# Bucketed attention and a gated feed-forward: the masks of two score blocks made in one step on row quarters of TensorE, with four score slots

## The chip, the cores and the metric

The kernel runs on one core of one Trainium2 chip. The core has TensorE (PE, matrix products; PEld is its loading of weights), VectorE (DVE), ScalarE (ACT), GpSimd (POOL) and SyncE (SP); the last two mostly issue transfers here. Matrix products read SBUF and write PSUM, which has eight banks of 2 KiB per partition. The metric is the device time of one execution in microseconds, the median of several.

## The reference

Attention in which a query sees only the keys that fall into the same hash bucket, and then a feed-forward block on the result:

```python
batch, n_heads, seq, head_dim = (4, 8, 768, 64)
...
q_bits = (np.einsum('bhsd,dk->bhsk', q, proj) > 0).astype(np.int64)      # proj: 64 x 6
k_bits = (np.einsum('bhsd,dk->bhsk', k, proj) > 0).astype(np.int64)
powers = 2 ** np.arange(n_bits)
q_bucket = np.sum(q_bits * powers, axis=-1)
k_bucket = np.sum(k_bits * powers, axis=-1)
mask = q_bucket[:, :, :, None] == k_bucket[:, :, None, :]
scores = scale * np.matmul(q, k.transpose(0, 1, 3, 2))
scores = np.where(mask, scores, -1000000000.0)
scores = scores - np.max(scores, axis=-1, keepdims=True)
attn = np.exp(scores)
attn = attn / (np.sum(attn, axis=-1, keepdims=True) + 1e-09)
return np.matmul(attn, v).astype(np.float32)
...
h = x @ w_in                                       # x: 3072 x 512, w_in: 512 x 2048
sp = np.maximum(h, 0.0) + np.log1p(np.exp(-np.abs(h)))
g = h * erf(sp)
return (g @ w_out).astype(np.float32)
```

## The kernel before

The kernel has two stages, attention and feed-forward, in one program. In each, a planner (`arrange`, L120) puts the operations in order before anything is emitted: every operation has an engine, a planned cost, a rank and a list of operations it comes after, and the planner plays the engines forward and emits each operation at its planned start. Each engine then works strictly in the order of emission; what one engine must wait for on another is put in as semaphores, from the tiles that an instruction reads and writes.

**Attention** takes the 32 heads in 16 runs of two heads each (`i`, `NPAIR` = 16). The two heads `ab` = 0, 1 lie on the lower and upper 64 partitions. A run has 2 halves of the queries (`HS` = 384 columns) and 6 blocks of 128 keys, so 12 score blocks; `n` = 4i + 2*half + g counts groups of `GC` = 3 blocks, `c` the block in a group.

- `score(n, c)` (L543, matrix products at L557) fills one slot `st`, a PSUM tile of two banks, one bank for each head. First the mask: for each head a bf16 product over 64 rows of `both` (the hashed bits of q and k as +1 and -1, with weights such that the product is 0 where all bits agree and hugely negative elsewhere; only 7 of the 64 rows are not zero). Then the float32 product of q and k, over 64 rows, on top of it. A float32 product is two instructions in the profile. The two heads' products use different halves of TensorE's rows and run at the same time.
- There are three such slots (`big`, `bufs=3`, six banks). `exponential(n, c)` (L581, ScalarE, L584) reads a slot and frees it. The slots also serve `bits_of` and `divisor`.
- `weigh(n)` (L632, products at L642) multiplies three blocks of exponentials with v; g = 0 and g = 1 of a half add up in one bank `av`. Half 0 has a bank of its own pool (`psum_v`), half 1 the single bank of the pool `misc`. `leave(h)` (L700, ScalarE, L708) copies a half out, `leave_plain(i)` (L710, VectorE, L714) reads one column of half 0.
- `bits_of(i + 2)` (L834, L845) hashes the pair that comes two runs later into the first bank of a slot; `divisor(i - 1)` (L670, L687) sums exponentials into the second bank of the same slot. `sign_of` (L853, L854), `weigh_bits`, `leave_bits` and `place_bits` (L876, L883) turn the hash into the rows of `both`: `leave_bits` writes them to DRAM and `place_bits` reads them back onto partitions ab*64 to ab*64+6 with two transfers, both issued on POOL. Runs 0 and 1 fill `both` in another way, all 64 rows used.
- `sum_keys` (VectorE, L630) adds up exponentials for the divisor. In between, VectorE and ScalarE convert the weights of the feed-forward (32 pieces, fetched on POOL's queue, L463; L477 to L539).

TensorE's order in attention is written out by hand in the list `order` (L906 to L918): for each run the twelve score blocks, the four `weigh`, then `bits_of(i + 2)` and `divisor(i - 1)`. The loop behind it (L920 to L944) gives each of them its planned cost and, with the list `slots`, the operation that frees the slot it takes:

```python
for c in range(GC):
    free = slots[-3] if len(slots) >= 3 else ()
    pe(score, (n, c), 0.82 if n or c == 2 else 0.17, after + free)
    slots.append((("exponential", n, c),))
```

**Feed-forward** (L1201) multiplies with w_in and w_out in a scheme with fewer products, applies the gate on ScalarE and VectorE, and takes `bank("X")` from the pool `misc`. `general()` (L1103) is a second version of attention for inputs whose scores are too large for the first; it isn't executed with these inputs.

Of the kernel before, what the change touches and what calls it, by code (L numbers as in the profile page):

```python
# [54 lines left out]
F32 = mybir.dt.float32  # L55
# [6 lines left out]
PSUM = bass.MemoryType.PSUM  # L62

P = 128
# [132 lines left out]
def kernel(  # L197
# [11 lines left out]
    nc = tc.nc  # L209
    B, H, S, D = v.shape  # L210
    NBIT = proj2.shape[1] // 2
# [4 lines left out]
    HS = S // 2  # L216
    JP = NPAIR // B
    GC = NC // 2
# [9 lines left out]

    const = ctx.enter_context(tc.tile_pool(name="const", bufs=1))
    dram = ctx.enter_context(tc.tile_pool(name="dram", bufs=2, space=bass.MemoryType.DRAM))  # L230
    misc = ctx.enter_context(tc.tile_pool(name="misc", bufs=1, space=PSUM))
    small = ctx.enter_context(tc.tile_pool(name="small", bufs=3))
    QR = 32
    QB = QR // 2
# [22 lines left out]
    for ab in range(2):  # L257
        rows = slice(ab * D, ab * D + D)
        nc.vector.tensor_copy(
            out=proj_sb[rows, ab * QR : ab * QR + NBIT],  # L260
            in_=proj_in[rows, ab * NBIT : (ab + 1) * NBIT],
        )
    row = const.tile([P, 1], F32, name="row")
    nc.gpsimd.dma_start(out=row, in_=bucket)
    steps = const.tile([P, 8], F32, name="steps")
    for c, (end, factor) in enumerate(
# [12 lines left out]
            out=steps[:, c : c + 1],  # L279
# [9 lines left out]
    for ab in range(2):  # L289
        rows = slice(ab * D, ab * D + D)  # L290
        nc.vector.tensor_copy(
            out=proj_q[rows, ab * QB : ab * QB + NBIT],
            in_=proj_in[rows, ab * NBIT : (ab + 1) * NBIT],
# [7 lines left out]
        nc.vector.memset(cq[:, j : j + 1], c)  # L301

    def bank(name):
        return misc.tile([P, 512], F32, name=name, tag="bank")

    WP = 512
    WIDE = w_in.dtype != F32
# [112 lines left out]
    def attention():  # L420
        NS = NPAIR * 4
        with (
# [10 lines left out]
            def big(name):  # L433
                return psum.tile([P, 2, 512], F32, name=name, tag="big", bufs=3)
# [9 lines left out]
            pairs = {}  # L444
# [80 lines left out]
            def add_rest(n):  # L525
# [14 lines left out]
                    out=pieces[n][0], in0=top[:, :].bitcast(F32), in1=rest, op=ALU.add  # L540
                )

            def score(n, c, parts=((0, "b"), (1, ""))):  # L543

                i, half, g = n // 4, n // 2 % 2, n % 2
                d = pairs[i]
                cols = slice(half * HS, (half + 1) * HS)
                keys = slice((g * GC + c) * P, (g * GC + c + 1) * P)
                if ("st", n, c) in d:
                    parts = ((1, "b"),)  # L550
                else:
                    d["st", n, c] = big("st")
                st = d["st", n, c]
                for part, src in parts:
                    for ab in range(2):
                        rows = slice(ab * D, ab * D + D)
                        nc.tensor.matmul(  # L557
                            out=st[:, ab, 0:HS],
                            lhsT=d["k" + src][rows, keys],
                            rhs=d["q" + src][rows, cols],  # L560
                            start=(part == 0),
                            stop=(part == 1),
                        )
# [68 lines left out]
            def weigh(n):  # L632
                half, g = n // 2 % 2, n % 2
                d = pairs[n // 4]
                if g == 0:
                    d["av", half] = bank("av") if half else psum_v.tile([P, 512], F32, name="av", tag="av")
                w = HS + 1 - half
                for c in range(GC):
                    e = block(n, c)
                    for ab in range(2):  # L640
                        rows = slice(ab * D, ab * D + D)
                        nc.tensor.matmul(  # L642
                            out=d["av", half][rows, 0:w],
                            lhsT=d["v"][:, g * GC + c, rows],
                            rhs=e[:, ab, 0:w],
                            start=(g == 0 and c == 0),
                            stop=(g == 1 and c == GC - 1),
                        )
# [153 lines left out]
                pairs[i] = fetch(i, load)  # L802

            pairs[0] = fetch(0, load, quick=True)
            warm = bank("warm")
            for n in range(WARM):
                nc.tensor.matmul(  # L807
                    out=warm[0:D, 0:P],
# [19 lines left out]
            def pe(fn, args, cost, after=()):  # L828
                if chain:
                    after += (chain[-1],)  # L830
                op(fn, args, "PE", cost, (0, len(chain)), after, late=0.25)
                chain.append((fn.__name__,) + args)
# [43 lines left out]
            def place_bits(i):  # L876

                d = pairs[i]
                bd = d.pop("bd")
                for n, what in enumerate(("qb", "kb")):  # L880
                    d[what] = both[i % 2][:, n, :]
                for ab in range(2):
                    nc.gpsimd.dma_start(  # L883
                        out=both[i % 2][ab * D : ab * D + NBIT + 1, :, :].rearrange(
                            "r w (h c) -> r (w h) c", h=2
                        ),
                        in_=bd[:, ab, 0 : NBIT + 1, :].rearrange("n r c -> r n c"),
                    )

            def place_first():  # L890

# [16 lines left out]
            for i in range(NPAIR):  # L908
# [7 lines left out]
                    order.append(("divisor", i - 1))  # L916
                if i == NPAIR - 2:
                    order.append(("divisor", i))  # L918
            slots = []
            for what, n in order:  # L920
                free = slots[-3] if len(slots) >= 3 else ()
                if what == "score":
                    i = n // 4
                    after = (("double_first",) if i == 1 else ("place_bits", i),)
                    for c in range(GC):
                        free = slots[-3] if len(slots) >= 3 else ()
                        pe(score, (n, c), 0.82 if n or c == 2 else 0.17, after + free)
                        slots.append((("exponential", n, c),))
                elif what == "bits":
                    pe(bits_of, (n,), 0.80 if n > 1 else 1.44, (("start_pair", n),) + free)  # L930
                    slots.append((("sign_of", n),) if n > 1 else (("place_first",),))
                elif what == "divisor":
                    if n != NPAIR - 3:
                        free = ()
                        slots[-1] += (("keep_divisor", n),)
                    else:
                        slots.append((("keep_divisor", n),))
                    pe(divisor, (n,), 0.72, (("sum_keys", n, last_sum(n)),) + free)
                else:
                    h = n // 2  # L940
                    after = (("exponential", n, GC - 1),)
                    if n % 2 == 0:
                        after += (("leave", h - 2), ("leave_plain", (h - 2) // 2))
                    pe(weigh, (n,), 2.0, after)  # L944
            sums_after = {}
            for i in range(NPAIR):
                for k, (_, blocks_) in enumerate(sum_steps(i)):
# [33 lines left out]
            for h in range(NH):  # L981
                i = h // 2
# [3 lines left out]
            for i in range(NPAIR):  # L986
                n = 4 * i
                if i:
                    op(
                        start_pair,  # L990
                        (i,),
                        "SP",
                        3.6,
                        (0, n - 6),
                        (("weigh", n - 9), ("bits_of", i - 1))
                        + tuple(("measure", i - 3, m, half) for m in range(2) for half in range(2)),
                        late=3.5,
                    )
                    if i == 1:
                        op(place_first, (), "ACT", 0.9, (0, n - 2, 9), (("bits_of", i),))  # L1000
                        for ab in (1, 0):
                            op(weigh_first, (ab,), "DVE", 0.43, (0, n - 2, 1), (("place_first",),))
                        op(double_first, (), "DVE", 0.35, (0, n - 2, 2), (("weigh_first", 0), ("weigh_first", 1)))
                    else:
                        op(sign_of, (i,), "ACT", 0.6, (0, n - 6, 9), (("bits_of", i), ("leave_bits", i - 1)))
                        op(weigh_bits, (i,), "DVE", 0.33, (0, n - 6, 1), (("sign_of", i),))
                        op(leave_bits, (i,), "POOL", 0.7, (0, n - 6, 2), (("weigh_bits", i),), late=4.0, far=True)
                        op(
                            place_bits,
                            (i,),  # L1010
                            "POOL",
                            1.2,
                            (0, n - 6, 3),
                            (("leave_bits", i), ("score", n - 5, 2), ("clean", i - 2)),
                            late=3.6,
                        )
# [86 lines left out]
    def general():  # L1103

        with (
# [3 lines left out]
            tc.tile_pool(name="ep", bufs=2) as ep,  # L1109
            tc.tile_pool(name="row", bufs=4) as small,  # L1110
            tc.tile_pool(name="psum", bufs=1, space=PSUM) as psum,
        ):

            def big(name):
                return psum.tile([P, 2, 512], F32, name=name, tag="big", bufs=3)
# [85 lines left out]
    def feed_forward(check, late):  # L1201
        again = late is None
        with (
# [4 lines left out]
            tc.tile_pool(name="wtp", bufs=2) as wtp,  # L1208
            tc.tile_pool(name="ps_f", bufs=1, space=PSUM) as ps_f,
            tc.tile_pool(name="ps_l", bufs=1, space=PSUM) as ps_l,  # L1210
        ):
            NTILE = NT // T
            NP = NTILE * NC4
            FILL = 3
# [618 lines left out]
```

## Time and profile before

| | us |
|---|---|
| median of 3 runs | 904.84 (904.79 to 905.12) |
| the profiled execution | 904.72 |
| its span, first to last instruction | 902.9 |
| attention, first score block of run 1 to first feed-forward product | 27.3 to 313.5 |
| one run, first mask to first mask | 19.13 in most |
| a run's score blocks: 12 | 9.7 |
| a run's weigh: 4 | 7.9 |
| bits_of and divisor | 0.67 and 0.77 |

The costliest groups of attention on the profile's page:

| line, engine | what | count | busy us |
|---|---|---|---|
| L557 PE | st from q, k (f32) | 768 | 155.1 |
| L557 PE | st from both (bf16 masks) | 384 | 63.5 |
| L642 PE | av from e_even; from area | 384; 360 | 65.6; 60.6 |
| L584 ACT | exponentials into e_even; into area | 96; 90 | 70.6; 68.0 |
| L630 DVE | sums of exponentials | 46 | 79.2 |
| L845 PE | bits from k; from q | 56; 56 | 11.8; 11.7 |

How to read the profile: it is one execution. A shape such as 64*128 in front of an operation of TensorE is the part of its array that the operation uses, rows by columns. Lengths of TensorE's instructions are modelled and overlap their neighbours, so the distance between two starts says more than a length. "Idle before" is the time an engine waited ahead of an instruction, and the name behind `<-` is what ended that wait.

### The profile page before, as it was taken

How to read it: one execution, taken by the hardware profiler on the slowest of the kernel's cores; microseconds unless marked ns; L12 is line 12 of the kernel's file. 1: busy time of each engine (PE TensorE's matmuls, PEld its weight loads, DVE VectorE, ACT ScalarE, POOL GpSimd, SP SyncE). 2: the span in 40 equal slices, each digit the busy share in tenths (PEclk: the TensorE clock that was granted, in tenths of full speed). 3: DMA queues.
4: the chain of work that ended last, by engine and by line, in shares of the span. 5: the costliest groups of instructions: out<-in, count | busy, mean ns of one | idle time of the engine just before them, and what ended most of it. 6: DMA issues, size and time to landing. Idle time of an engine off the chain costs nothing.

```text
span 902.9 us, 12780 instructions
## 1 busy us (share of the span) xinstructions
PE 894.3 (99%) x5016; PEld 670.9 (74%) x5016; DVE 668.5 (74%) x837; ACT 563.3 (62%) x808; POOL 57.9 (6%) x95
## 2 busy tenths in 40 slices
PE   9999999999999999999999999999999999999997
PEld 5455554455544588888888888888888888888886
DVE  5999999999999879995666556666776666655652
ACT  6788888788886668855645455545655555545520
POOL 1211211111110000000000001000100010000000
PEclk9999999999999999999999999999999999999999
DMA  9547655667551322202231013211421122111211
GB/s 228 149 128 183 200 166 142 196 173 195 154 157 60 101 89 65 82 36 70 59 106 58 14 49 103 82 36 47 105 83 36 36 74 78 35 36 57 63 68 50
DMA packets 65156, 86.82 MB, mean 96 GB/s; under 512 B 34364, under 2 KB 47772, under 8 KB 65088
## 3 DMA queue, kind: packets, MB, share of 16 engines
q1 hardware_dynamic: 56528, 63.81, 24.8%
q0 software_dynamic: 8112, 21.66, 8.6%
q8 instruction: 41, 0.67, 0.3%
q10 hardware_dynamic: 448, 0.46, 0.2%
q14 instruction: 27, 0.22, 0.1%
HBM read 64.67 MB, written 17.30 MB: 91 GB/s over the span
## 4 chain that ended last, share of the span: by engine, by line
PE 99%; DVE 0%; issue 0%; ACT 0%; DVEq 0%
PE M L1361 32%; PE X L1248 29%; PE st L557 17%; PE av L642 14%; PE M L1248 3%; PE bits L845 1%; PE bits L687 1%; PE warm L807 0%; PE bits L377 0%; PE z_ps L687 0%; DVE e L1288 0%; DVE h L1270 0%; ACT both L390 0%; DVE u L1396 0%; DVE norms L1754 0%
## 5 line engine op out<-in xcount | busy, mean ns | idle before, releaser
L1288 DVE SCALAR_TENSOR_TENSOR e<-w,e 128x1024 f32<-128x1024 f32 x144 | 173.7, 1220 | 8.4 <-ACT w L1282 3.9
L1248 PE MATMUL X<-area,w_in_sb 128*128 128x256 f32 x680 | 160.6, 379 | 0.0
L1282 ACT ACTIVATE w<-h,cq 128x1024 f32<-128x1024 f32 x144 | 155.6, 1136 | 0.1
L557 PE MATMUL st<-q,k 64*128 64x384 f32 x768 | 155.1, 482 | 0.0
L1270 DVE TENSOR_TENSOR h<-X,h 128x512 f32<-128x512 f32 x65 | 44.8, 689 | 144.4 <-PE X L1248 144.4
L1248 PEld LDWEIGHTS X<-area,w_in_sb 128*128 128x128 f32 x680 | 129.2, 190 | 17.6
L1361 PE MATMUL M<-w_out_sb,h 128*128 128x256 f32 x576 | 141.1, 379 | 0.0
L1248 PE MATMUL X<-area 128*128 128x256 f32 x520 | 122.8, 379 | 0.0
L1361 PEld LDWEIGHTS M<-w_out_sb,h 128*128 128x128 f32 x576 | 109.4, 190 | 14.9
L1266 ACT COPY h<-X 128x512 f32<-128x512 f32 x85 | 49.3, 580 | 111.4 <-PE X L1248 111.3
L1248 PEld LDWEIGHTS X<-area 128*128 128x128 f32 x520 | 98.8, 190 | 13.4
L1278 ACT ACTIVATE e<-h,cq 128x1024 f32<-128x1024 f32 x48 | 55.1, 1148 | 85.9 <-DVE h L1270 85.8
L1361 PE MATMUL M<-wt,S 128*128 128x256 f32 x384 | 95.1, 379 | 0.0
L557 PEld LDWEIGHTS st<-q,k 64*128 64x128 f32 x768 | 68.8, 187 | 29.7 <-issue 27.2
L630 DVE TENSOR_TENSOR area<-area 128x1536 f32<-128x1536 f32 (+1 forms) x46 | 79.2, 1723 | 7.5 <-ACT area L584 6.3
L1361 PEld LDWEIGHTS M<-wt,S 128*128 128x128 f32 x384 | 73.0, 190 | 9.9
L584 ACT ACTIVATE e_even<-st 128x768 f32<-128x768 f32 x96 | 70.6, 822 | 0.4 <-PE st L557 0.3
L584 ACT ACTIVATE area<-st 128x768 f32<-128x768 f32 x90 | 68.0, 817 | 0.0
L642 PE MATMUL av<-e_even,v 128*64 128x385 f32 x384 | 65.6, 490 | 0.0
L557 PE MATMUL st<-both 64*128 64x384 bf16 x384 | 63.5, 323 | 0.3 <-ACT both L390 0.3
L1303 DVE TENSOR_TENSOR h<-h,e 128x1024 f32<-128x1024 f32 x48 | 57.9, 1220 | 4.6 <-ACT e L1299 4.6
L642 PE MATMUL av<-area,v 128*64 128x384 f32 x360 | 60.6, 486 | 0.0
(129 smaller groups left out, 976.8 us busy)
## 6 DMA issues: line engine op xcount, KB each, us to landing
wt<-wt SPq DMA_DIRECT2D x24, 768.0 KB, 4.2
raw<-in_w_out_dram POOLq DMA_DIRECT2D x16, 512.0 KB, 4.2
raw<-in_w_in_dram POOLq DMA_DIRECT2D x14, 512.0 KB, 4.6
v<-in_v_dram SPq DMA_DIRECT2D x32, 192.0 KB, 4.6
q<-in_qkT_dram SPq DMA_DIRECT2D x30, 192.0 KB, 4.2
k<-in_qkT_dram SPq DMA_DIRECT2D x30, 192.0 KB, 4.7
r<-rd SPq DMA_DIRECT2D x30, 192.0 KB, 3.7
xs<-x SPq DMA_DIRECT2D x15, 384.0 KB, 3.0
```

The source lines that it names most:

```text
L557: nc.tensor.matmul(out=st[:, ab, 0:HS], lhsT=d["k" + src][rows, keys], rhs=d["q" + src][rows, cols], start=(part == 0), stop=(part == 1),)
L584: nc.scalar.activation(out=e[:, :, 0:HS], in_=st[:, :, 0:HS], func=AF.Exp, scale=scale)
L630: nc.vector.tensor_tensor(out=into, in0=one, in1=two, op=ALU.add)
L642: nc.tensor.matmul(out=d["av", half][rows, 0:w], lhsT=d["v"][:, g * GC + c, rows], rhs=e[:, ab, 0:w], start=(g == 0 and c == 0), stop=(g = ...
L1248: nc.tensor.matmul(out=d[where][:, u, :], lhsT=a[:, kc, f : f + P], rhs=b[:, kc, :], start=(first and u == 0 and kc == 0), stop=(last and ...
L1266: nc.scalar.copy(out=quarter(p, q), in_=st[p][where])
L1270: nc.vector.tensor_tensor(out=h, in0=st[p][where], in1=h, op=ALU.add)
L1278: nc.scalar.activation(out=s, in_=unit(p, v), func=AF.Sigmoid, bias=cq[:, n : n + 1])
L1282: nc.scalar.activation(out=q, in_=unit(p, v), func=AF.Sigmoid, scale=GATE_S[j][0], bias=cq[:, j : j + 1])
L1288: nc.vector.scalar_tensor_tensor(out=s, in0=st[p].pop(("q", v, j)), scalar=GATE_S[j][2], in1=s, op0=ALU.add, op1=ALU.mult,)
L1303: nc.vector.tensor_tensor(out=h, in0=h, in1=st[p].pop(("s", v)), op=ALU.mult)
L1361: nc.tensor.matmul(out=banks[name][:, sub, :], lhsT=a[:, u, sub * P : (sub + 1) * P], rhs=b[:, u, :], start=(c == 0 and k == 0), stop=(c = ...
```

## The change

Masks for runs 2 to 15 are made by a new function `mask`, for two blocks at once: `place_bits` now puts the seven rows of bits twice onto each head's 64 partitions, at offset 0 and at offset 32 (`QR`), with four transfers; `mask` uses the first copy for the one block and the second for the other, as four bf16 products over 32 rows each, into the four banks of two slots. It is called ahead of blocks 0, 2, 4, 6 and 8 of a run (`QUARTERS`), and `score` then finds the slot filled and adds only q times k. Blocks 10 and 11, and all of runs 0 and 1, keep the mask in `score` over 64 rows; in blocks 10 and 11 of runs 2 to 15 both copies of the bits take part.

The two single banks of attention become a fourth slot of two banks, `psum_v` with the tag `side`. Blocks 3 and 7 of a run take it, and then `weigh`: both halves of `av` are now the two banks of one such tile. The pool `misc` with its single bank is opened inside `general` and `feed_forward` instead of at the start. The hand-written order of TensorE is the same but for the new `mask` operations; `free_of` works out which operation frees a slot, now for two rings. Planned costs change: 0.655 for a score without its mask, 0.22 for `mask`, 0.70 for bits, 1.98 for `weigh`, 2.4 for `place_bits`.

```diff
-    misc = ctx.enter_context(tc.tile_pool(name="misc", bufs=1, space=PSUM))
+    single = []
...
     def bank(name):
-        return misc.tile([P, 512], F32, name=name, tag="bank")
+        return single[-1].tile([P, 512], F32, name=name, tag="bank")
...
+            SIDE = (3, 7)
+            QUARTERS = tuple(range(0, 10, 2))
+
+            def place(n, c):
+
+                return n // 4, n % 4 * GC + c
+
+            def slot_of(n, c):
+                if place(n, c)[1] in SIDE:
+                    return psum_v.tile([P, 2, 512], F32, name="st", tag="side")
+                return big("st")
+
+            def mask(n, c):
+
+                i, at = place(n, c)
+                d = pairs[i]
+                for m in range(2):
+                    n, c = 4 * i + (at + m) // GC, (at + m) % GC
+                    half, g = n // 2 % 2, n % 2
+                    cols = slice(half * HS, (half + 1) * HS)
+                    keys = slice((g * GC + c) * P, (g * GC + c + 1) * P)
+                    st = d["st", n, c] = slot_of(n, c)
+                    for ab in range(2):
+                        rows = slice(ab * D + m * QR, ab * D + (m + 1) * QR)
+                        nc.tensor.matmul(
+                            out=st[:, ab, 0:HS],
+                            lhsT=d["kb"][rows, keys],
+                            rhs=d["qb"][rows, cols],
+                            start=True,
+                            stop=False,
+                        )
+
             def score(n, c, parts=((0, "b"), (1, ""))):
...
                 if ("st", n, c) in d:
-                    parts = ((1, "b"),)
+                    parts = ((1, "b" if i == 0 else ""),)
                 else:
-                    d["st", n, c] = big("st")
+                    d["st", n, c] = slot_of(n, c)
...
                 if g == 0:
-                    d["av", half] = bank("av") if half else psum_v.tile([P, 512], F32, name="av", tag="av")
+                    if not half:
+                        d["avs"] = psum_v.tile([P, 2, 512], F32, name="av", tag="side")
+                    d["av", half] = d["avs"][:, half, :]
...
-                for ab in range(2):
-                    nc.gpsimd.dma_start(
-                        out=both[i % 2][ab * D : ab * D + NBIT + 1, :, :].rearrange(
-                            "r w (h c) -> r (w h) c", h=2
-                        ),
-                        in_=bd[:, ab, 0 : NBIT + 1, :].rearrange("n r c -> r n c"),
-                    )
+                for m in range(2):
+                    for ab in range(2):
+                        row = ab * D + m * QR
+                        nc.gpsimd.dma_start(
+                            out=both[i % 2][row : row + NBIT + 1, :, :].rearrange(
+                                "r w (h c) -> r (w h) c", h=2
+                            ),
+                            in_=bd[:, ab, 0 : NBIT + 1, :].rearrange("n r c -> r n c"),
+                        )
...
-            slots = []
+            slots, side = [], []
+
+            def free_of(*sides):
+                at = {True: len(side), False: len(slots)}
+                gone = ()
+                for is_side in sides:
+                    ring, room = (side, 1) if is_side else (slots, 3)
+                    if at[is_side] >= room:
+                        gone += ring[at[is_side] - room]
+                    at[is_side] += 1
+                return gone
+
             for what, n in order:
-                free = slots[-3] if len(slots) >= 3 else ()
                 if what == "score":
                     i = n // 4
-                    after = (("double_first",) if i == 1 else ("place_bits", i),)
+                    ready = (("double_first",) if i == 1 else ("place_bits", i),)
                     for c in range(GC):
-                        free = slots[-3] if len(slots) >= 3 else ()
-                        pe(score, (n, c), 0.82 if n or c == 2 else 0.17, after + free)
-                        slots.append((("exponential", n, c),))
+                        at = place(n, c)[1]
+                        free = free_of(at in SIDE)
+                        cost = 0.82 if n or c == 2 else 0.17
+                        if i > 1 and at in QUARTERS:
+                            pe(mask, (n, c), 0.22, ready + free_of(at in SIDE, at + 1 in SIDE))
+                        if i > 1 and at <= QUARTERS[-1] + 1:
+                            cost = 0.655
+                        pe(score, (n, c), cost, ready + free)
+                        (side if at in SIDE else slots).append((("exponential", n, c),))
...
                     h = n // 2
                     after = (("exponential", n, GC - 1),)
-                    if n % 2 == 0:
-                        after += (("leave", h - 2), ("leave_plain", (h - 2) // 2))
-                    pe(weigh, (n,), 2.0, after)
+                    if n % 4 == 0:
+                        after += free_of(True)
+                        side.append((("leave", h), ("leave_plain", h // 2), ("leave", h + 1)))
+                    pe(weigh, (n,), 1.98, after)
...
                             place_bits,
                             (i,),
                             "POOL",
-                            1.2,
+                            2.4,
```

More of the change, by code (lines that the diff above doesn't have):

```diff
@@ L804, in attention @@
             pairs[0] = fetch(0, load, quick=True)
-            warm = bank("warm")
+            warm = big("warm")[:, 0, :]
             for n in range(WARM):
@@ L918, in attention @@
                     order.append(("divisor", i))
-            slots = []
+            slots, side = [], []
[8 more added lines that the diff above has]
+                return gone
             for what, n in order:
-                free = slots[-3] if len(slots) >= 3 else ()
                 if what == "score":
                     i = n // 4
-                    after = (("double_first",) if i == 1 else ("place_bits", i),)
+                    ready = (("double_first",) if i == 1 else ("place_bits", i),)
                     for c in range(GC):
-                        free = slots[-3] if len(slots) >= 3 else ()
-                        pe(score, (n, c), 0.82 if n or c == 2 else 0.17, after + free)
-                        slots.append((("exponential", n, c),))
+                        at = place(n, c)[1]
[7 more added lines that the diff above has]
+                        (side if at in SIDE else slots).append((("exponential", n, c),))
                 elif what == "bits":
-                    pe(bits_of, (n,), 0.80 if n > 1 else 1.44, (("start_pair", n),) + free)
+                    pe(bits_of, (n,), 0.70 if n > 1 else 1.44, (("start_pair", n),) + free_of(False))
                     slots.append((("sign_of", n),) if n > 1 else (("place_first",),))
                 elif what == "divisor":
+                    free = ()
                     if n != NPAIR - 3:
-                        free = ()
                         slots[-1] += (("keep_divisor", n),)
                     else:
+                        free = free_of(False)
                         slots.append((("keep_divisor", n),))
@@ L1111, in general @@
             tc.tile_pool(name="psum", bufs=1, space=PSUM) as psum,
+            tc.tile_pool(name="misc", bufs=1, space=PSUM) as misc,
         ):
+            single.append(misc)
             def big(name):
@@ L1210, in feed_forward @@
             tc.tile_pool(name="ps_l", bufs=1, space=PSUM) as ps_l,
+            tc.tile_pool(name="misc", bufs=1, space=PSUM) as misc,
         ):
+            single.append(misc)
             NTILE = NT // T
```

## The prediction

> **What bounds the kernel now.** I read the page first: its busy times and the chain of work that ended last.
>
> ```profile
> span 902.9 us, 12780 instructions
> PE 894.3 (99%) x5016; PEld 670.9 (74%) x5016; DVE 668.5 (74%) x837; ACT 563.3 (62%) x808; POOL 57.9 (6%) x95
> ...
> PE 99%; DVE 0%; issue 0%; ACT 0%; DVEq 0%
> ```
>
> TensorE is busy from end to end and is 99% of the chain. So a microsecond of TensorE time that is removed or added anywhere moves the end by a microsecond, as long as no other engine is late. The sum is therefore made over TensorE, against the span of 902.9 us. What lies around it is 904.72 - 902.9 = 1.8 us in the profiled execution, which is 0.12 us under the median, 904.84; I carry 1.9 us.
>
> Next I read the timeline of TensorE over one whole run (a pair of heads). Columns: start, length, engine, line, operation, tiles, shape, count. Lengths are modelled and overlap, so I use differences of starts.
>
> ```profile
> 150.54 0.33 PE L557 MATMUL st<-both 64*128 64x384 bf16 x2
> 150.70 0.81 PE L557 MATMUL st<-q,k 64*128 64x384 f32 x4
> 151.35 0.33 PE L557 MATMUL st<-both 64*128 64x384 bf16 x2
> 151.51 0.81 PE L557 MATMUL st<-q,k 64*128 64x384 f32 x4
> 152.25 4.10 PE L642 MATMUL av<-e_even,v 128*64 128x385 f32 x24
> 156.18 4.04 PE L642 MATMUL av<-area,v 128*64 128x384 f32 x24
> 160.15 0.52 PE L845 MATMUL bits<-q,proj_q 128*32 128x384 f32 x2
> ...
> 160.50 0.49 PE L845 MATMUL bits<-q,proj_q 128*32 128x384 f32 x2
> ...
> 160.82 0.83 PE L687 MATMUL bits<-area,ones 128*32 128x192 f32 x16
> 161.59 0.34 PE L557 MATMUL st<-both 64*128 64x384 bf16 x2
> 161.76 0.81 PE L557 MATMUL st<-q,k 64*128 64x384 f32 x4
> ```
>
> A block's mask takes 0.16 us (150.54 to 150.70), its q·k product 0.65 (150.70 to 151.35). After the last product weigh starts 0.74 later, not 0.65: **a change of tiling costs 0.09** (the shape in front, 64*128 to 128*64). The other changes agree: divisor to the next mask (160.82 to 161.59) is 0.77, where its 16 instructions, four groups of half as many columns as bits' (0.32 a group, 160.50 to 160.82), last 4 x 0.16 = 0.64: 0.1 more. The first operation behind a change is longer too: the first mask 0.17 (161.59 to 161.76), +0.01. For f32 weights of 128 columns it is much more, and the start of the kernel shows that:
>
> ```profile
> 6.11 1.56 PE L557 MATMUL st<-q,k 64*128 64x384 f32 x8
> 7.60 0.54 PE L377 MATMUL bits<-q,proj_sb 128*64 128x384 f32 x1
> ```
>
> Two products between two changes take 1.49 = 2 x 0.65 + 0.09 (the change at their end) + 0.10 (the first of them). That is the price of a q·k product straight behind a change.
>
> Last I read the other engines, by the windows of one run and by two of their rows.
>
> ```profile
> core 0: us, PE busy (x) PEld busy (x) DVE busy (x) ACT busy (x) POOL busy (x), PEclk, DMA share, GB/s
> ...
> 84.70:103.90 19.20, 19.20 (x150) 9.65 (x148) 18.48 (x26) 15.14 (x28) 3.36 (x6) 1.00 0.66 178
> ```
> ```profile
> L854 ACT ACTIVATE sg<-bits,sgn 128x384 bf16<-128x384 f32 x14 | 8.1, 581 | 11.8 <-PE bits L687 11.5 <-PE bits L845 0.3
> ```
> ```profile
> 156.40 0.48 ACT L708 COPY x<-av 128x384 f32<-128x384 f32 x1 [0.66 <-PE av L642]
> ```
> ```profile
> 157.38 0.15 DVE L714 TENSOR_SCALAR ev<-av 128x1 f32<-128x1 f32 x1
> ```
>
> VectorE is busy 18.48 of a run's 19.20 us, ScalarE 15.14; the granted clock is 1.00. The row of L854 matters most. sign_of reads the first bank of the tile bits, which L845 wrote. It idles 11.5 us until **L687**, the divisor, which writes the other bank of the same tile and stands between the two in program order. So a reader of one bank here waits for an earlier write to the other bank: dependencies of a two-bank tile go by the whole tile.
>
> **The change, part by part.**
>
> *Masks on row quarters* (runs 2 to 15, so 14; five pairs each). Four instructions of 64 rows in two steps become four of 32 rows in one: 5 x 0.16 = 0.80 us a run saved, as many weight loads as before. But the stream, until now 64*128 through all twelve blocks, changes to 32*128 and back. Entries: the first pair's takes the place of the change after the divisor, so four are new, 4 x (0.09 + 0.01) = 0.40. Exits: five, each in front of a product, 5 x (0.09 + 0.10) = 0.95. Net 0.40 + 0.95 - 0.80 = +0.55 a run, **+7.7 us** over 14. No row shows a change of rows alone. Nearest rows: every change in this trace, whichever dimension changes, costs about 0.09, so one end of the bound is +7.7; the other is a change for nothing, -0.80 x 14 = -11.2. I take the first because no row has a free change.
>
> The Trainium skill says the same of rows that no trace here shows ("TensorEngine Tiling (Array Packing)", Key Properties): changing the tiling mode, not just the tile, drains the engine, and it lists 64 and 32 rows as different modes. By it the sum is +7.7; by the trace alone it stays between -11.2 and +7.7.
>
> That four tiles run together at full pitch I take from bits, four column tiles every 0.32 (160.50 to 160.82).
>
> The skill's "TensorE: Matmul & The Clock Gate" (Part 3, Measured speedup vs the span model) has 3.07 instead of 4 for four row tiles; by it a mask would take 0.16 x 4 / 3.07 = 0.21, an estimate, and 70 of them 3.5 us more.
>
> *Both halves of av in one two-bank tile* (all 16 runs). On TensorE weigh(4i+2) follows weigh(4i+1) at once, while leave and leave_plain, which read half 0, can only start after weigh(4i+1). So in program order weigh(4i+2) comes ahead of these reads and weigh(4i+3) behind them. Before, that was harmless: two tiles. By L854's row the reads of half 0 now wait for weigh(4i+2) (bank 1), and, if the rule holds from reader to writer as it does from writer to reader, weigh(4i+3) waits for the reads. With T as half 1's first matmul (156.18): weigh(4i+2) ends at T + (160.15 - 156.18 - 0.09)/2 = T + 1.94. The copy now starts 0.22 behind T (156.40), so then at T + 2.16, ends at T + 2.64; leave_plain, 0.15, reads the same bank and follows or precedes it: T + 2.8, some 0.05 to reach TensorE. Stall 2.85 - 1.94 = 0.9 us a run, **+14.4 us**. Nearest rows bound it: 0 if banks are told apart in this direction; above, VectorE now reaches leave_plain up to 1.2 us behind T here (157.38), so it adds nothing, and I allow 1.1 x 16 = 17.6 for runs in which it is later. I take 0.9 because the only row of this kind waits by the tile.
> Queued behind: on ScalarE, which waits in order, the squares of the weights (0.66 idle ahead of leave now, about 2.6 then, out of 19.20 - 15.14 = 4 spare); on VectorE the weight conversion loses 2.66 - 1.2 = 1.5 us a run, 18.48 + 1.5 = 20.0, under the new run of 19.15 + 0.55 + 0.9 = 20.6. If that cover were gone (no change of tiling paid, run 19.25) VectorE would be late by up to 0.7 us in the eight runs where it is fullest, some 3 us with the slack later.
>
> *Four slots.* A pair's mask needs two free slots 0.65 earlier than the second block did. The tightest are blocks 5 and 11. Exponentials come every 0.73 us (2.90 for four in ScalarE's timeline), a pair of blocks every 1.62 + 0.11 = 1.73 with the changes, so ScalarE gains on TensorE: cost 0, hidden by that. Were changes free (1.46 a pair), TensorE would wait up to 0.4 us a run at block 11. The side slot is asked for by the next run's block 3 some 3 us after weigh ends (bits 0.67, divisor 0.77, first pair 1.6); leave needs 0.7 of that: 0.
>
> *place_bits* issues four DMAs instead of two: 2 x 0.57 us more on POOL's queue (POOL is busy 3.36 of 19.20) and 2.5 us to landing, the median of the 28 now. The bits are asked for about 10 us later (placed at 167.2, next run at 180.7): 0. The weight fetches queued behind them move by 1.1 us; the square that reads a fetched piece now idles 0.0 us for it: 0. Planner costs, the masks' stripes read twice by blocks 10 and 11, and the bank pool moved to the second part change no instruction's length: 0.
>
> Sum: 902.9 + 7.7 + 14.4 = 925.0, + 1.9 = **926.9 us**.
>
> **The rivals.**
> 1. *The stall without the changes of tiling* (a row change is free). 902.9 - 11.2 + 14.4 + 3 (VectorE) + 1.9 = 911. For: TensorE's stream keeps 128 columns, and no row forbids it. Against: no free change anywhere.
> 2. *The changes without the stall* (banks told apart when a write follows a read). 902.9 + 7.7 + 1.9 = 912.5. For: the reader's wait of L854 is no proof for a writer. Against: one rule for both is the simpler reading.
> 3. *Faster: neither.* Decided by one mechanism, the price of entering and leaving 32-row tiling: below 0.80/9 = 0.09 us for each of a run's nine new changes the masks gain, and with no stall that is the end. Free, -11.2; VectorE, 18.5 busy against 18.35, keeps some 0.4 in eight runs: -8. 902.9 - 8 + 1.9 = 897. For: the four masks themselves are surely 0.16 instead of 0.32. Against: both rows above.
> That the masks would not share a step (four row tiles one after another) would add 0.16 to each pair, 70 x 0.16 = 11 us to any of these; bits speaks against it.
>
> **How the numbers follow.** Forecast 0.42 (919 to 931, by 0.6 to 1.1 of stall and one change more or less), rival 1 0.27 (905 to 915), rival 2 0.11 (907 to 914), rival 3 0.17 (893 to 903), anything else 0.03. The range 900 to 931 leaves out the better part of rival 3 and a few hundredths above. 0.2% is 1.8 us, about what a measurement of this kernel can tell from no change: faster is rival 3 with a little of rival 1, 0.19; same 0.03; slower 0.78.
>
> **What would show it.** Tiling: between the last product of a pair and the next mask 0.74, from mask to product 0.26, the first product of a pair 0.75 and the second 0.65; if 0.65, 0.16, 0.65, rival 1 or 3. Stall: an idle gap of about 0.9 us on TensorE in the middle of av's second half, ended by ScalarE L708 or VectorE L714, once a run, and the first leave 2.2 us behind T instead of 0.2; without that gap, rival 2 or 3. Wrong altogether: TensorE waiting for exponentials, or for the bits' DMA at a run's start.

## The result and the profile after

The changed kernel takes 929.91 us (median of 4, 929.16 to 930.73) where the kernel before takes 904.82 (904.77 to 905.12): a ratio of 1.0277 with a 95% interval of 1.0259 to 1.0295, 25.1 us slower. The prediction was 927, range 900 to 931.

The page of the changed kernel, its span, busy times and the chain by engine:

```profile
span 928.0 us, 12795 instructions
...
PE 906.4 (98%) x5016; PEld 657.6 (71%) x5016; DVE 668.4 (72%) x837; ACT 568.7 (61%) x808; POOL 73.1 (8%) x123
...
PE 96%; DVE 2%; ACT 1%; issue 0%; DVEq 0%
```

The span grew by 25.1 us, TensorE's busy time by 12.1, though no matrix product was added (x5016 as before). So TensorE works longer on the same instructions, and it also stands idle; VectorE and ScalarE, which had 0% of the chain, now hold 2% and 1% of it. As lengths are modelled, how much falls to each is better read from starts. The timeline of TensorE over one run shows both (start, length, engine, line, operation, tiles, shape, count, idle time before):

```profile
152.97 0.34 PE L567 MATMUL st<-both 32*128 32x384 bf16 x4
153.24 1.56 PE L589 MATMUL st<-q,k 64*128 64x384 f32 x8
154.74 0.34 PE L567 MATMUL st<-both 32*128 32x384 bf16 x4
155.01 1.56 PE L589 MATMUL st<-q,k 64*128 64x384 f32 x8
...
160.03 0.34 PE L567 MATMUL st<-both 32*128 32x384 bf16 x4
...
161.70 0.33 PE L589 MATMUL st<-both 64*128 64x384 bf16 x2
161.86 0.81 PE L589 MATMUL st<-q,k 64*128 64x384 f32 x4
162.50 0.33 PE L589 MATMUL st<-both 64*128 64x384 bf16 x2
162.67 0.81 PE L589 MATMUL st<-q,k 64*128 64x384 f32 x4
163.41 4.10 PE L676 MATMUL av<-e_even,v 128*64 128x385 f32 x24
167.34 2.11 PE L676 MATMUL av<-area,v 128*64 128x384 f32 x12
170.22 2.16 PE L676 MATMUL av<-area,v 128*64 128x384 f32 x12 [0.77 <-DVE ev L748]
172.30 0.52 PE L879 MATMUL bits<-q,proj_q 128*32 128x384 f32 x2
...
173.74 0.34 PE L567 MATMUL st<-both 32*128 32x384 bf16 x4
```

A pair of blocks takes 1.765 us (four of them from 152.97 to 160.03); two blocks with a mask each took 2 x 0.81 = 1.62. The last two blocks, with masks over 64 rows, keep their 0.81 (161.70 to 162.50). Twelve blocks: 163.41 - 152.97 = 10.44, before 9.79 (the 9.7 of the table of before is twelve times 0.81, without the change of tiling at their end). Then the second half of av: its two parts start 2.88 apart (167.34, 170.22), before 1.93, and the idle time before the second is ended by VectorE's ev. From there to bits it is 2.08 (170.22 to 172.30), before 2.04. A run is 173.74 - 152.97 = 20.77 us long, before 19.13.

TensorE's waits for these two readers (total us, times, longest) are 14 and 2, one in each of the 16 runs; the kernel before has no such wait:

```profile
PE av L676 <- DVE ev L748: 11.3, 14, 1.3
PE av L676 <- ACT x L742: 1.3, 2, 0.8
```

What happens on the other engines in that gap, ScalarE first, then VectorE, then TensorE's loading of weights:

```profile
169.49 0.48 ACT L742 COPY x<-av 128x384 f32<-128x384 f32 x1 [2.21 <-PE av L676]
```
```profile
170.00 0.16 DVE L748 TENSOR_SCALAR ev<-av 128x1 f32<-128x1 f32 x1 [2.73 <-ACT x L742]
```
```profile
170.21 0.20 PEld L676 LDWEIGHTS av<-area,v 128*64 128x64 f32 x4 [1.44 <-DVE ev L748]
```

The copy of half 0 starts 2.15 us behind the first matmul of half 1 (167.34), where it started 0.22 behind it before: it waited for the third weigh, which writes the other bank. ev follows the copy, and the fourth weigh follows ev by 0.06 us (170.00 + 0.16 to 170.22). Its first weights, too, are loaded only then (170.21), which goes with the 0.05 us that this weigh takes longer (2.086 instead of 2.037 before rounding).

### The profile page after: what moved, and what is told of

The parts are those of the page before. It is cut to its first block, busy times and chain, and to the rows that moved or that the text cites. A ratio compares the mean times of both kernels' runs of the same rounds, so it can differ in the third digit from the quotient of the medians.

```text
span 928.0 us, 12795 instructions
## 1 busy us (share of the span) xinstructions
PE 906.4 (98%) x5016; PEld 657.6 (71%) x5016; DVE 668.4 (72%) x837; ACT 568.7 (61%) x808; POOL 73.1 (8%) x123
## 4 chain that ended last, share of the span: by engine, by line
PE 96%; DVE 2%; ACT 1%; issue 0%; DVEq 0%
PE M L1419 31%; PE X L1306 28%; PE st L589 15%; PE av L676 13%; PE M L1306 3%; PE st L567 2%; PE bits L879 1%; DVE area L662 1%; PE bits L721 1%; ACT x L742 1%; PE warm L841 0%; PE bits L377 0%; DVE ev L748 0%; PE z_ps L721 0%; DVE e L1346 0%
## 5 line engine op out<-in xcount | busy, mean ns | idle before, releaser
L589 PE MATMUL st<-q,k 64*128 64x384 f32 x768 | 151.2, 502 | 0.0
L589 PEld LDWEIGHTS st<-q,k 64*128 64x128 f32 x768 | 66.8, 186 | 41.2 <-issue 22.8
L676 PE MATMUL av<-area,v 128*64 128x384 f32 x360 | 63.9, 490 | 11.9 <-DVE ev L748 10.5
L676 PEld LDWEIGHTS av<-area,v 128*64 128x64 f32 x360 | 24.6, 136 | 48.6 <-issue 26.7
```

The source lines that it names most:

```text
L589: nc.tensor.matmul(out=st[:, ab, 0:HS], lhsT=d["k" + src][rows, keys], rhs=d["q" + src][rows, cols], start=(part == 0), stop=(part == 1),)
L676: nc.tensor.matmul(out=d["av", half][rows, 0:w], lhsT=d["v"][:, g * GC + c, rows], rhs=e[:, ab, 0:w], start=(g == 0 and c == 0), stop=(g = ...
```

## The experiments

Seven kernels were run. The first four ran on one chip, the last three on another; the kernel before, run beside them on the same chip, took 904.48 us with the first four and 904.77 with the last three. Each ratio is to that.

**The leaves late.** The reads of half 0 move behind the last write of the same tile.

```diff
-op(leave, (h,), "ACT", 0.48, (0, 2 * h, -2), (("weigh", 2 * h + 1), ("send", i - 3)))
+op(leave, (h,), "ACT", 0.48, (0, 2 * h, -2), (("weigh", 4 * i + 3), ("send", i - 3)))
...
-    op(leave_plain, (i,), "DVE", 0.15, (0, 2 * h, 0), (("weigh", 2 * h + 1),))
+    op(leave_plain, (i,), "DVE", 0.15, (0, 2 * h, 0), (("weigh", 4 * i + 3),))
```

> After, but leave and leave_plain of half 0 come after the fourth weigh of the run instead of the second, so that no read of av's first bank stands between two writes of its second bank. The masks on row quarters stay. Theory (a stall of 0.95 us a run, 16 runs, by the wait of a whole tile): 929.9 - 15.2 = 915, no idle time of TensorE ahead of av's second half. Rival (the stall is VectorE being late with its own work): it comes back elsewhere, 925 or more.

Measured: 917.99 us (ratio to before 1.0146, 1.0129 to 1.0163). The stall is gone from every run: the two parts of av's second half start 1.93 apart, as before, and a run lasts 19.77. But 918 is 3 more than expected, and from the last matmul of av to the end it takes 595.0 us, where the kernel before takes 589.8. TensorE's timeline at the start of the feed-forward, VectorE's, and the windows there (length, busy time of PE, PEld, DVE, ACT, POOL, granted clock, DMA share and rate):

```profile
321.73 3.72 PE L1306 MATMUL M<-area,w_in_sb 128*128 128x256 f32 x16
328.69 5.38 PE L1306 MATMUL M<-area 128*128 128x256 f32 x16 [3.24 <-DVE area L346]
```
```profile
325.28 1.94 DVE L807 SCALAR_TENSOR_TENSOR x<-x,ev,r 128x768 f32<-128x768 f32 x2
327.14 2.61 DVE L346 TENSOR_TENSOR area<-area 128x512 f32<-128x512 f32 x4
```
```profile
322.00:326.00 4.00, 3.46 (x16) 2.69 (x15) 3.22 (x5) 1.29 (x3) 0.00 (x0) 1.00 0.01 2
326.00:328.00 2.00, 0.00 (x0) 0.00 (x0) 1.97 (x4) 0.00 (x0) 0.00 (x0) 1.00 0.43 167
328.00:330.00 2.00, 1.31 (x5) 1.15 (x6) 2.00 (x4) 0.00 (x0) 0.00 (x0) 0.84 0.58 226
330.00:332.00 2.00, 2.00 (x6) 1.56 (x5) 1.93 (x3) 0.18 (x1) 0.00 (x0) 0.50 0.00 0
```

TensorE waits 3.24 us for L346, the first sums of x on VectorE, which is full in that stretch (1.97 of 2.00): the last of the weights' work and the scaling of the last results (L807) stand ahead of L346 in its order. Then the granted clock is 0.50 for a while, and sixteen matmuls take 5.38 us, where the sixteen ahead of the gap took 3.72. The rival, the stall coming back in the runs, falls; the tail is a cost of its own, taken up below.

**The masks as before.** The four slots, the shared tile and the early leaves stay, the masks go back to 64 rows.

```diff
-            QUARTERS = tuple(range(0, 10, 2))
+            QUARTERS = ()
...
-                        if i > 1 and at <= QUARTERS[-1] + 1:
+                        if i > 1 and at in QUARTERS:
```

> After, but with the mask of every block over 64 rows again; the four slots, av as two banks of one tile and the early leaves stay. Theory: what is left is the stall, 904.8 + 15.2 = 920, and the masks' share is 929.9 - 920 = 10. Rival (the masks cost nothing, everything is the stall): 929 or so.

Measured: 920.85 us (1.0178, 1.0161 to 1.0195). Twelve blocks take 9.79 us again, and the two parts of av's second half are still 2.88 apart. The rival falls: the stall alone is not the whole loss.

**The slots alone.** Both of these edits together.

> After, with the masks over 64 rows again and the leaves after the fourth weigh: only the four slots, the shared tile of av and the doubled DMAs of the bits are left of the change. Theory: both costs gone, 905 (904 to 906.5). Rival (the slots or the DMAs cost something): over 907.

Measured: 904.02 us (0.9992, 0.9982 to 1.0001), with the kernel before at 904.48: no difference that ten runs can tell. TensorE waits for a slot, the leaves or the bits in no run; its 0.3 us for the very first signs are there before, too.

**A change of tiling for every block.** The price of the change by itself, in the kernel before.

```diff
-                        rows = slice(ab * D, ab * D + D)
+                        rows = slice(ab * D, ab * D + (QR if src and i > 1 else D))
```

> Before, but every mask of runs 2 to 15 over 32 rows instead of 64 (the bits fill 7 of them), one block at a time: the same instructions, and a change of rows ahead of and behind each of the 12 masks of a run. Theory (each change drains TensorE, 0.093 at its end, a head of 0.012 for the mask and 0.104 for the product): 11 x 0.105 + 12 x 0.197 = 3.52 us a run, x 14 = 49: 954. Rival (a change of rows alone is free and the pair's cost has another cause, such as four tiles sharing a step badly): 905.

Measured: 953.85 us (1.0543, 1.0522 to 1.0564), two runs. The end of a run's blocks in this kernel's timeline:

```profile
149.47 0.34 PE L557 MATMUL st<-both 32*128 32x384 bf16 x2
149.73 0.92 PE L557 MATMUL st<-q,k 64*128 64x384 f32 x4
150.58 4.10 PE L642 MATMUL av<-e_even,v 128*64 128x385 f32 x24
```

The same two masks of 0.16 us now take 0.26 up to the product, and the product 0.85 up to the next change: 1.11 a block where it was 0.81. Twelve blocks take 13.36, which is 3.57 more, where 3.52 was expected. Only rows change here, and only two tiles share a step, so neither a free change of rows nor trouble among four tiles can explain the price.

**The plan with true costs.** The leaves-late kernel, with the planner told what the masks cost.

```diff
-pe(mask, (n, c), 0.22, ready + free_of(at in SIDE, at + 1 in SIDE))
+pe(mask, (n, c), 0.35, ready + free_of(at in SIDE, at + 1 in SIDE))
...
-                            cost = 0.655
+                            cost = 0.70
```

> The leaves late with the masks on row quarters, but the planner is told what the masks really cost (0.35 a pair's mask and 0.70 a product instead of 0.22 and 0.655). Theory (the 5 us that the leaves-late kernel loses at the start of the feed-forward come from VectorE's order, planned for a shorter run, so that the first sums of x are late by 3.2 us and the clock drops after that gap): the gap goes, 904.0 + 14 x 0.64 = 913. Rival (the tail comes from the late leaves themselves): 917 or more.

Measured: 913.05 us (1.0091, 1.0076 to 1.0107). The runs are the same 19.77 us, the gap ahead of the feed-forward's sums is gone, and from the last matmul of av to the end it takes 589.0. So the 5 us came from the planned order, fixed in advance for a run that doesn't exist; the wait that went with it is the one for VectorE's L346. This is also the clean price of the masks: 913.05 - 904.02 = 9.0 us, or 8.7 if each is first taken against the kernel before on its own chip (8.28 more and 0.46 less); the length of the runs gives 14 x 0.64 = 9.0.

**Only leave early.** The changed kernel with leave_plain alone behind the fourth weigh.

```diff
-    op(leave_plain, (i,), "DVE", 0.15, (0, 2 * h, 0), (("weigh", 2 * h + 1),))
+    op(leave_plain, (i,), "DVE", 0.15, (0, 2 * h, 0), (("weigh", 4 * i + 3),))
```

> After, but only leave_plain on VectorE comes after the fourth weigh; ScalarE's leave of half 0 stays behind the second. Theory (the stall is ScalarE's copy, 0.22 to its start and 0.48 long, and then VectorE's one-column read behind it, which waits for the copy since both read one bank): TensorE now waits for the copy alone, 0.75 us a run instead of 0.95, 929.9 - 3 = 927, and the wait is put down to ACT L742. Rival (VectorE's lateness alone makes the stall): 915 to 918.

Measured: 925.79 us (1.0235, 1.0219 to 1.0250). The two parts of av's second half start 2.68 apart in every run, 0.75 more than without a stall, and the waits of TensorE name the copy (total us, times, longest):

```profile
PE av L676 <- ACT x L742: 8.6, 15, 0.6
```

So of the 0.94 us, 0.75 are ScalarE's copy and 0.19 VectorE's read behind it. The time is 1.2 under the expected 927; one reason is that the feed-forward is shorter as well: from the last matmul of av to the end it takes 589.1, in the changed kernel 590.1. VectorE being late with other work, the rival, would have left 915 to 918.

**One step saved.** What the prices point to: a mask on quarters where a change is paid anyway, left again through a bf16 mask. The edit is against the slots alone.

```diff
-            SIDE = (3, 7)
-            QUARTERS = ()
+            SIDE = (2, 7)
+            QUARTERS = (0,)
...
+            def early(n, c):
+
+                score(n, c, ((0, "b"),))
...
-                            pe(mask, (n, c), 0.22, ready + free_of(at in SIDE, at + 1 in SIDE))
-                        if i > 1 and at in QUARTERS:
+                            pe(mask, (n, c), 0.17, ready + free_of(at in SIDE, at + 1 in SIDE))
+                            pe(early, (n, c + 2), 0.27, ready + free_of(True))
+                        if i > 1 and at < 3:
```

> The slots alone (leaves after the fourth weigh), but with the masks on row quarters for blocks 0 and 1 only, straight behind the divisor, where a change of tiling is paid anyway, and then block 2's mask over 64 rows before any product, so that the second change is met by a bf16 mask (head 0.012) and not by a float32 product (head 0.104). Block 2 takes the side slot instead of block 3. Theory: a run saves 0.162 and pays 0.093 + 0.012 = 0.057 less, x 14 = 0.8: 903.2 where the slots alone are 904.0, and 0.7 to 1.3 under before. Rival (the early third slot makes TensorE wait for the leaves of the run before): 905 or more, with idle time ahead of block 2.

Measured: 903.65 us (0.9990, 0.9981 to 0.9999), eleven runs. Its timeline at the start of a run:

```profile
160.98 0.34 PE L567 MATMUL st<-both 32*128 32x384 bf16 x4
161.25 0.34 PE L589 MATMUL st<-both 64*128 64x384 bf16 x2
161.43 2.10 PE L589 MATMUL st<-q,k 64*128 64x384 f32 x12
163.36 0.33 PE L589 MATMUL st<-both 64*128 64x384 bf16 x2
```

Three blocks take 163.36 - 160.98 = 2.38 us, where three ordinary ones at a run's start take 0.01 + 3 x 0.808 = 2.43. Runs 3 to 14 last 19.08 instead of 19.13; run 2 lasts 19.30. The kernel is a little under the one before (904.77 on this chip); between it and the slots alone (904.02 on the other chip) the times don't decide, only the length of the run in the profile does.

## Why the prediction was right, point by point

**The bound** held: every microsecond on TensorE came out at the end. Nine new changes of tiling and one stall a run are nearly the whole difference. The forecast of 926.9 is 3.0 under the measured 929.91, which lies 1.1 under the upper end of the range. Both terms of the sum were too small, the masks by 0.7 us and the stall by 1.8, and 0.5 stood in no term; that they err to the same side is why the time is so near that end.

**Masks on row quarters.** The step was +0.55 us a run; it is 10.435 - 9.794 = 0.64, in 14 runs 9.0 us instead of 7.7. In the two profiles the blocks differ by 8.4, since in the one of before five runs have blocks longer than 9.80, by 0.04 to 0.29 and 0.6 in all, for a reason that stays open. Every part was as named (entry, exit, expensive first product); only the sizes were a little off. Rounded starts gave 1.75 for a pair (0.26 + 0.75 + 0.74) and 1.62 for the two blocks that it replaces; they are 1.765 and 1.616, and five such differences are the missing 0.09. Most of it lies from mask to product, 0.27 instead of 0.26: the change is nearer 0.10 than 0.09. That a change of rows alone is a full change, which no row of the profile before showed, is shown by the kernel with a change at every block. The rule of the Trainium skill that was weighed for it ("TensorEngine Tiling (Array Packing)", Key Properties: a changed mode drains the engine) agrees, with 0.10 us for each. The 3.07-fold speed of four row tiles, the other figure weighed ("TensorE: Matmul & The Clock Gate", Part 3, there with 512 columns), does not show: from mask to product it takes 0.27 with four tiles and 0.26 with two (the kernel with a change at every block), where that figure would add 0.05, an estimate.

**The stall by the shared tile.** Predicted 0.9 us a run, measured 0.94 in most (2.876 - 1.933); with one run of 1.46 and one of 0.75 the 16 add up to 15.4 us, 14.4 predicted. A second part was put at nothing without a word: the fourth weigh, its weights not loaded ahead, takes 0.05 longer, 0.8 us in 16 runs. That makes 16.2. (The 0.77 us of idle time in the profile are less than 0.94 because the modelled end of the third weigh reaches into the gap.) The chain was the one described: third weigh, copy, one-column read, fourth weigh. The leaves-late kernels, which take away only the interleaving of reads and writes, remove it, the 0.05 included. The sum of the profile is 8.4 + 16.2 = 24.6 of the 25.1 us by which the span grew; of the rest 0.2 lie ahead of the first masks and 0.3 in the feed-forward.

**The four slots and place_bits at nothing** held: the kernel that keeps just these is within 0.2% of before.

**VectorE under cover** held, with more room than thought: it waits 2.73 us ahead of ev in the run shown and is still no bound. What the prediction missed there is the start of the feed-forward: once the stall is taken away, an order planned for shorter runs costs 5 us (917.99 - 913.05). In the changed kernel itself the stall covers it: from the last matmul of av to the end it takes 590.1 there.

**The rivals.** The stall without the changes (911) and the changes without the stall (912.5) were priced as what remains when one of the two is free. The second of them exists as a kernel, 913.05. Faster needed a change under 0.09 us; it costs 0.10, and 0.20 with the slower first product behind it. On its own terms the edit's first idea, two masks in one step, gains: 0.16 us a pair. The gain is spent on entering and leaving the quarters.

The two costs add up: 904.02 + 9.0 + 16.8 (920.85 - 904.02) = 929.8 against 929.91. So neither hides behind the other.

What stays open: whether the waits follow the whole tile or a coarser range of addresses was not tried; these runs can't tell them apart, and both give the same waits here.

## What to carry to other kernels

Before an operation is packed into quarters of TensorE, count the changes of tiling that it puts into the stream and what stands behind each: here a step saved was worth 0.16 us, a change cost 0.10, and 0.20 when a float32 product with 128 weight columns came next. Two results that are read at different times belong in two PSUM tiles, or the reads belong behind the last write: a free bank is no independence if the wait is made for the tile. And when an order is planned in advance, a planner told of costs that the chip doesn't have can lose time far from the change: here 5 us at the start of the feed-forward.

## What the runs showed of the hardware that the profile before did not

A change of rows alone (64 to 32 of them, same columns) costs TensorE as much as any other change, 0.10 us, though only two of the array's tiles were in use. The first float32 product behind it (128 weight columns) takes another 0.10, a bf16 mask 0.01; the first float32 product with 64 weight columns behind a wait takes 0.05 more (the fourth weigh). After an idle gap of 3.24 us the mean granted clock was 0.84 and then 0.50 in windows of 2 us; it fell only some 0.7 us after TensorE had begun to work again, was 0.50 from 329.4 to 332.7, and 1.00 again from 332.8 on. So the gap cost some 5 us in all, 3.24 idle and 5.38 - 3.72 slower. The stalls of 0.77 us, once in 20.8 us, left the clock at 1.00.
